# State tokens: the high and low moving parts side by side in one 512-column matmul

## The chip, the cores and the metric

The kernel runs on one NeuronCore of a Trainium2 chip. The metric is the device time of one execution in microseconds. Three runs of the kernel before gave 1387.56, 1388.13 and 1390.54 us; their median is 1388.13 us. TensorE (PE) does the matmuls, ScalarE (ACT) and VectorE (DVE) read PSUM and work in SBUF, GpSimd (POOL) works in SBUF, SyncE (SP) issues the DMAs. PEld is TensorE's loading of weights.

## The reference

Two attention reads (tokens over a state, and the state over the tokens) are joined to 8 x 544 tokens of 512 features: for each of 8 batch entries 512 ordinary tokens and 32 state tokens. Two gated layers follow.

```python
def _attn_ref(x, state):              # x 8,8,512,64; state 8,8,32,64
    a = softmax(scale * x @ state^T);   xread = a @ state
    a2 = softmax(scale * state @ x^T);  sread = a2 @ x
    return concatenate([xread, sread], axis=2)
def _moe_ref(x, w_gate, w_val, w_out):        # 512 -> 1536 -> 512
    gate = 1.0 / (1.0 + exp(-(x @ w_gate)))
    return (gate * (x @ w_val)) @ w_out
def _moe2_ref(x, w_in, w_out):                # 512 -> 2048 -> 512
    h = x @ w_in
    g = where(h >= 1, h, where(h <= -1, 0, (h + 1)**2 / 4))
    return g @ w_out
```

The 8 x 32 = 256 state tokens go through the same two layers as the 4096 others; in the kernel they are block `B` (number 8), beside blocks 0 to 7 of 512 tokens each.

## The kernel before

All matrix products are made in a reduced 32-bit type. Each factor is split into a high part (rounded, an ACT copy) and a low part (the rest, a subtraction), and a product is three matmuls that add up in PSUM: high weights by high values, high weights by low values, low weights by high values (`mm3`, lines 213 to 218, and the same three in `out1`, lines 769 to 771). Every matmul has its own load of 128x128 weights. An ordinary block gives 512 moving columns to a matmul, which fills a PSUM bank; the state block gives 256 and half a bank.

The state block appears in four places, and the change touches the first three.

- **First layer, gate and value** (`emit_g1s`, 12 units m): 8 terms of `mm3` write the two banks of one PSUM tile; then ACT takes the sigmoid of one bank (line 845), DVE multiplies by the other (846), and ACT and DVE split the product into high and low (128, 129).
- **First layer, output** (`out1` with b = 8, 12 units): 4 terms of three matmuls into four accumulating banks. `state_block` runs these units between ordinary blocks 6 and 7: it emits `emit_g1s(m)` and its eviction, and then the output of unit m - 2 (`LAG`). After unit 11, ACT copies two banks out and DVE the other two (lines 776, 778), and SP stores them.
- **Second layer, input** (`unit_s`, 8 units, four in each of two state blocks "s"): two banks of 4 terms each; each bank then goes through ACT relu, ACT square, and DVE min/max which reads the bank once more (`act_g2`, lines 1083 to 1087).
- The second layer's output for the state tokens uses other loops, which stay as they are.

Instructions run on each engine in the order in which the program emits them. The second layer's input runs over ten blocks (ordinary 0, 1, 2, state, ordinary 3, and this twice, for two halves of the hidden units). An ordinary block has 4 units (`unit`), each of seven products of six 512-column matmuls in the order `PO` = M1, M6, M5, M7, M2, M3, M4. They use four banks, u0 to u3, of two buffers each: M1 in u0, M6 in u1, M5 in u2, M7 in u3; M2 adds on top of M1's bank, M3 on M5's, M4 on M7's (line 1108). ACT copies M1's bank to SBUF after M1 (line 1133), and VectorE's sums follow from that copy. `unit_s` takes its two banks from u0 and u1, so the unit two places further on has to wait until a bank has been read. A tick after each product or half unit issues planned work of other blocks, such as the ACT copy of 128x1024 values that makes the high part of the next block (line 1044) and the POOL subtraction that makes the low part (1047).

Of the kernel before, what the change touches and what calls it, by code (L numbers as in the profile page):

```python
# [8 lines left out]
F32 = mybir.dt.float32  # L9
F32R = mybir.dt.float32r  # L10
U32 = mybir.dt.uint32
I32 = mybir.dt.int32
AF = mybir.ActivationFunctionType
ALU = mybir.AluOpType
# [11 lines left out]
def attention_moe_moe_kernel(  # L26
# [28 lines left out]
    nc = tc.nc  # L55

    ctx.enter_context(tc.manual_schedule())
    B, H, S, D = x.shape
# [5 lines left out]
    NM1 = F1 // 128  # L64
    NM2 = F2 // 128
    NQ = NM1 // 2
    NSB = B * N
    HP = H // 2
    SCALE = 1.0 / float(D) ** 0.5
    LAG = 2  # L70
# [11 lines left out]
    def ps_tile(k):  # L82
        return psets[k].tile([128, 2, 512], F32, tag="ps", name=f"ps{k}")
# [26 lines left out]
    xs_dram = tc.dram_tile([128, 4, NSB], F32, name="xs_dram")  # L110
    wf_dram = [tc.dram_tile([128, 512], F32, name=f"wf_dram_{i}") for i in range(4 * NQ)]
    ws_dram = [tc.dram_tile([128, 4, 2, 512], F32, name=f"ws_dram_{q}") for q in range(NQ)]
    y_dram = [
        tc.dram_tile([128, 4, S if j < B else NSB], F32, name=f"y_dram_{j}")
        for j in range(B + 1)
    ]
# [7 lines left out]
    def f32(ap):  # L124
        return ap.bitcast(F32)

    def split(hi, lo, src):
        nc.scalar.activation(out=hi, in_=src, func=AF.Copy)
        nc.vector.tensor_tensor(out=lo, in0=src, in1=f32(hi), op=ALU.subtract)
# [83 lines left out]
    def mm3(ps, terms):  # L213
        n = len(terms)
        for i, (wh, wl, vh, vl) in enumerate(terms):
            nc.tensor.matmul(out=ps, lhsT=wh, rhs=vh, start=(i == 0), stop=False)
            nc.tensor.matmul(out=ps, lhsT=wh, rhs=vl, start=False, stop=False)
            nc.tensor.matmul(out=ps, lhsT=wl, rhs=vh, start=False, stop=(i == n - 1))

    xa_t, xT_t, sc_t, t_t, e2_t, r2_t = {}, {}, {}, {}, {}, {}
    at_t, a_t = {}, {}
# [475 lines left out]
    wo_t = {}  # L699
# [22 lines left out]
    hr_t, h_t, acc_t = {}, {}, {}  # L722
# [36 lines left out]
    def out1(b, m, hi, lo, n, os):  # L759
        k = b % 2  # L760
        if m == 0 and os[0] == 0:
            acc_t[1, b] = [ps_tile(k) for _ in range(2)]
        acc = acc_t[1, b]
        wh, wl = wo_t[m]
        for o in os:
            c = slice(128 * o, 128 * o + 128)
            first, last = m == 0, m == NM1 - 1
            ps = acc[o // 2][:, o % 2, :n]
            nc.tensor.matmul(out=ps, lhsT=wh[:, c], rhs=hi, start=first, stop=False)  # L769
            nc.tensor.matmul(out=ps, lhsT=wh[:, c], rhs=lo, start=False, stop=False)  # L770
            nc.tensor.matmul(out=ps, lhsT=wl[:, c], rhs=hi, start=False, stop=last)  # L771
        if m == NM1 - 1 and os[-1] == 3:
            for i in range(2):
                evv = ev_tile(i)[:, :, :n]
                if i == 0:
                    nc.scalar.activation(out=evv, in_=acc[i][:, :, :n], func=AF.Copy)
                else:
                    nc.vector.tensor_copy(evv, acc[i][:, :, :n])
                nc.sync.dma_start(out=y_dram[b][:, 2 * i : 2 * i + 2], in_=evv)

    def ev_tile(i):
        if b_last:
            return hp_.tile([128, 2, 512], F32, tag=("xs_hi", "xs_lo")[i], name="ev1")
        return evp.tile([128, 2, 512], F32, tag="ev1", name="ev1", bufs=2)

    b_last = False

    def output1(bg, slot, between=None):

# [42 lines left out]
    def emit_g1s(m):  # L832
        q, mm = m // 2, m % 2
        t = ws_t[q]
        ps = ps_tile(1)
        for v in range(2):
            c = slice(256 * v + 128 * mm, 256 * v + 128 * mm + 128)
            mm3(
                ps[:, v, :NSB],
                [(t[:, r, 0, c], t[:, r, 1, c], xs_hi[:, r], xs_lo[:, r]) for r in range(4)],  # L840
            )

        def evac():
            sg = hsp.tile([128, NSB], F32, tag="sgs", name="sgs", bufs=2)
            nc.scalar.activation(out=sg, in_=ps[:, 0, :NSB], func=AF.Sigmoid)
            nc.vector.tensor_tensor(out=sg, in0=sg, in1=ps[:, 1, :NSB], op=ALU.mult)
            hi = hsp.tile([128, NSB], F32R, tag="hs_hi", name="hs_hi", bufs=3)
            lo = hsp.tile([128, NSB], F32R, tag="hs_lo", name="hs_lo", bufs=3)
            split(hi, lo, sg)
            h_t[1, B, m] = (hi, lo)  # L850

        return evac

# [5 lines left out]
    def tt(eng, o, a, b, op=SUB):  # L859
        eng.tensor_tensor(out=o, in0=a, in1=b, op=op)  # L860
# [219 lines left out]
    def act_g2(o, s, c):  # L1080


        nc.scalar.activation(out=s, in_=c, func=AF.Relu, bias=half, scale=0.5)  # L1083
        nc.scalar.activation(out=s, in_=s, func=AF.Square)  # L1084
        return lambda: nc.vector.scalar_tensor_tensor(  # L1085
            out=o, in0=s, scalar=1.0, in1=c, op0=ALU.min, op1=ALU.max
        )
# [10 lines left out]
    def u_bank(k):  # L1098
        return psu.tile([128, 512], F32, tag=f"u{k}", name=f"u{k}", bufs=2)
# [62 lines left out]

    def unit_s(m, tick):
        w = w_t[m]
        ps = [u_bank(e)[:, :NSB] for e in range(2)]
        bt = st_t["raw_c"].rearrange("p l (k f) -> p l k f", k=4)
        dt = st_t["d_c"].rearrange("p l (k f) -> p l k f", k=4)
        for e in range(2):
            terms = ((M5, bt, 0), (M4, dt, 0)) if e else ((M1, bt, 0), (M2, bt, 2))
            mm3(  # L1170
                ps[e],
                [
                    tuple(w[:, l, WI[j], 128 * k : 128 * k + 128] for l in range(2))
                    + (y[:, 0, o + k], y[:, 1, o + k])
                    for j, y, o in terms
                    for k in range(2)
                ],
            )
            if e == 0:
                tick(0)  # L1180
        late(None)
        sg = tmp.tile([128, 2, NSB], F32, tag="sg", name="sg", bufs=4)
        for e in range(2):
            act_g2(sg[:, e], sg[:, e], ps[e])()
        tick(1)
        puts.append(store_g2(B, m, sg))

# [223 lines left out]
    for w in PRE:  # L1411
        c, n = w[0], int(w[1:]) if w[1:].isdigit() else 0
# [212 lines left out]
    while wsq:  # L1625
# [8 lines left out]

    st_sb = ExitStack()
    hp_ = pool("hp1", side="right", stack=st_wo)
    xs_hi, xs_lo = (
        hp_.tile([128, 4, NSB], F32R, tag=f"xs_{n}", name=f"xs_{n}") for n in ("hi", "lo")
    )
    nc.sync.dma_start(out=f32(xs_lo), in_=xs_dram)  # L1640
    evp = hsp = pool("hsp", side="right", stack=st_sb)
    wsps = [pool("wsp", side="right", stack=st_sb)]
    st_e = ExitStack()
# [10 lines left out]

    def slot2(n, k):
        if n == 10:
            nc.scalar.activation(out=xs_hi, in_=f32(xs_lo), func=AF.Copy)
            tt(nc.vector, xs_lo, f32(xs_lo), f32(xs_hi))
        if 8 <= n < 72 and n % 8 == 0:
            load_ws((n - 8) // 32, (n - 8) // 8 % 4)  # L1660
        if n < 70:
            if n % 2 == 0 and n >= 6 and wi_steps:
                wi_steps.pop(0)()
        elif n == 70:
            st_g.close()
            wsps.append(pool("wsp2", stack=st_g))
        elif n < 72:
            for j in range(4):
                load_ws(2, j)
        elif early:  # L1670
            early.pop(0)()

    def state_block(b):
        nonlocal b_last, wtp
        if b != 6:
            return
        assert not wi_steps
        for m in range(NM1 + LAG):
            if m < 2:
                for j in range(2):  # L1680
                    load_ws(3, 2 * m + j)
            elif m < 6 and m % 2 == 0:
                for j in range(4):
                    load_ws(m // 2 + 3, j)
            evac = emit_g1s(m) if m < NM1 else None
            if evac:
                evac()
            if m >= LAG:
                hi, lo = h_t.pop((1, B, m - LAG))
                out1(B, m - LAG, hi, lo, NSB, (0, 1, 2, 3))  # L1690
        st_sb.close()
        st_g.close()
        b_last = True
        wtp = pool("wtp")
        hcps.append(pool("hcp0"))
        pe = pool("yce", stack=st_e)
        y_pools.update({i: pe for i in range(3)})
        loads, sums = load_y(0, nc.vector)
        ld, wh, wl = (
            [lambda m=m, f=f: f(m) for m in range(4)] for f in (load_wi, high_wi, low_wi)  # L1700
        )
        h3 = splits_y(0, range(7), nc.vector)[:3]
        yh = [lambda f=f: lows.append(f()) for f in h3]
        yl = lambda: lows.pop(0)()
        early.extend([*ld[:2], *loads, ld[2], wh[0], lambda: (wl[0](), ld[3]()), wh[1], wl[1]])
        early.extend([lambda: None, *sums, wh[2], yh[0], wl[2], wh[3], wl[3]])
        early.extend([lambda: (yh[1](), yl()), lambda: (yh[2](), yl()), yl])
# [16 lines left out]
    tmp = pool("tmp", side="right")  # L1724
# [179 lines left out]
```

## Time and profile before

| | |
|---|---|
| median of 3 runs | 1388.13 us (1387.56 to 1390.54) |
| the profiled execution | 1390.13 us |
| its span, first to last instruction | 1388.3 us |
| PE busy in the span | 1365.3 us (98%) |
| DVE, ACT, POOL busy | 886.7, 740.4, 263.4 us |
| mean granted TensorE clock | 0.998 of full speed |

Busy time of an engine is the time in which at least one of its instructions runs. Matmuls overlap, so the cost of one in a row of matmuls is the distance from one start to the next, not the duration that the profile gives it. Line numbers (L216) are those of the kernel before.

### The profile page before, as it was taken

To read this page: it belongs to the slowest core of one execution; us is meant where nothing else is said; L and a number is where in the kernel's file an instruction comes from. 1 tells how busy PE (TensorE), PEld (TensorE's weight loads), DVE (VectorE), ACT (ScalarE), POOL (GpSimd) and SP (SyncE) were. 2 spreads that over 40 slices of the span, in tenths; PEclk is the share of its full clock that TensorE was granted. 3 is DMA by queue.
4 is the path that set the end of the run, shared out by engine and by line. 5 is a ranking of instruction groups with operands and counts; after the bars stand their busy time and mean duration, and the time that the engine had idled before them with its cause. 6 is when DMAs were issued, how large, how long until landed. Compare 5 with 4: busy or idle time off the path is not lost. (4 is left out here: it accounts for less than half of the span.)

```text
span 1388.3 us, 23228 instructions
## 1 busy us (share of the span) xinstructions
PE 1365.3 (98%) x9028; PEld 1163.6 (84%) x9028; DVE 886.7 (64%) x1296; ACT 740.4 (53%) x1097; POOL 263.4 (19%) x163
## 2 busy tenths in 40 slices
PE   7999999999999999999999999999999999999997
PEld 5677788787777778889888888888889999999997
DVE  6667676684455454542486656666578887877775
ACT  7655556664544442321367787787875343434432
POOL 3100000000000000000047787797740000000000
PEclk9999999999999999999999999999999999999999
DMA  8387897969766858897665559966378344343333
GB/s 265 124 285 252 283 310 236 310 220 334 241 224 257 298 216 283 334 338 272 225 235 196 204 192 326 329 227 250 134 255 325 122 132 143 123 151 122 121 109 92
DMA packets 151998, 315.58 MB, mean 227 GB/s; under 512 B 13136, under 2 KB 80720, under 8 KB 150352
## 3 DMA queue, kind: packets, MB, share of 16 engines
q1 hardware_dynamic: 150536, 312.79, 64.5%
q8 instruction: 71, 1.16, 0.4%
q10 hardware_dynamic: 1352, 1.31, 0.3%
q14 instruction: 39, 0.32, 0.1%
HBM read 183.50 MB, written 130.55 MB: 226 GB/s over the span
## 5 line engine op out<-in xcount | busy, mean ns | idle before, releaser
L1125 PE MATMUL u<-yc,wt 128*128 128x512 f32 x1344 | 305.5, 389 | 0.3 <-DVE sg L1103 0.3
L1125 PEld LDWEIGHTS u<-yc,wt 128*128 128x128 f32 x1344 | 252.0, 188 | 52.9 <-DVE sg L1103 0.7
L615 PE MATMUL ps<-at_hi,M 128*128 128x512 f32 x768 | 243.5, 393 | 0.5 <-ACT at_hi L394 0.5
L615 PEld LDWEIGHTS ps<-at_hi,M 128*128 128x128 f32 x768 | 144.1, 188 | 49.9 <-issue 19.3
L860 POOL TENSOR_TENSOR w2c<-w2c 128x256 f32<-128x256 f32 (+2 forms) x40 | 40.3, 1022 | 682.3 <-DMA w2c<-w_dram 670.9
L615 PE MATMUL ps<-at_lo,M 128*128 128x512 f32 x384 | 149.9, 390 | 1.8 <-DVE at_lo L399 1.8
L769 PE MATMUL ps<-oh_hi,wo 128*128 128x512 f32 x368 | 147.1, 400 | 0.0
L770 PE MATMUL ps<-oh_lo,wo 128*128 128x512 f32 x368 | 143.7, 390 | 0.2 <-DVE oh_lo L738 0.2
L771 PE MATMUL ps<-oh_hi,wo 128*128 128x512 f32 x368 | 143.5, 390 | 0.0
L1193 PE MATMUL o<-wt,hc 128*128 128x256 f32 x476 | 135.0, 284 | 1.4 <-DVE cu L1324 0.8
L1195 PE MATMUL o<-wt,hc 128*128 128x256 f32 x476 | 134.8, 283 | 0.7 <-DVE hc L1242 0.7
L1195 PE MATMUL o<-w,hc 128*128 128x256 f32 x476 | 134.9, 283 | 0.0
L1193 PE MATMUL o<-w,hc 128*128 128x256 f32 x476 | 134.7, 283 | 0.0
L1194 PE MATMUL o<-w,hc 128*128 128x256 f32 x476 | 134.7, 283 | 0.0
L1194 PE MATMUL o<-wt,hc 128*128 128x256 f32 x476 | 134.7, 283 | 0.0
L1238 ACT ACTIVATE hc<-hc 128x512 fp32r<-128x512 f32 (+1 forms) x108 | 64.9, 603 | 130.2 <-DMA hc<-hd_dram 120.4
L600 DVE TENSOR_TENSOR M<-ps,M 128x1024 fp32r<-128x1024 f32 x48 | 56.6, 1219 | 99.7 <-ACT M L594 99.7
L1047 POOL TENSOR_TENSOR yc<-yr,yc 128x1024 fp32r<-128x1024 f32 x49 | 116.5, 2420 | 4.4 <-ACT yc L1044 4.3
L1085 DVE SCALAR_TENSOR_TENSOR sg<-u,sg 128x512 f32<-128x512 f32 x96 | 66.3, 691 | 68.1 <-ACT u L1084 67.3
L1238 ACT ACTIVATE hc<-hs 128x512 fp32r<-128x512 f32 (+1 forms) x144 | 80.0, 598 | 52.7 <-DVE hs L1235 52.1
L738 DVE TENSOR_TENSOR oh_lo<-oh_lo,oh_hi 128x1024 fp32r<-128x1024 f32 x48 | 58.6, 1223 | 73.7 <-ACT oh_hi L736 73.6
L1083 ACT ACTIVATE u<-sg,half 128x512 f32<-128x512 f32 x96 | 66.5, 692 | 67.1 <-DVE sg L1103 65.1
(165 smaller groups left out, 2755.9 us busy)
## 6 DMA issues: line engine op xcount, KB each, us to landing
hd_dram<-sg SPq DMA_DIRECT2D x64, 512.0 KB, 5.2
h_dram<-sg SPq DMA_DIRECT2D x48, 512.0 KB, 4.0
oh_lo<-h_dram SPq DMA_DIRECT2D x48, 512.0 KB, 6.0
hc<-hd_dram SPq DMA_DIRECT2D x96, 256.0 KB, 4.2
yr<-y_dram SPq DMA_DIRECT2D x32, 512.0 KB, 6.6
wraw<-in_moe_w_out_dram SPq DMA_DIRECT2D x28, 512.0 KB, 5.4
ws_dram<-w SPq DMA_DIRECT2D x24, 512.0 KB, 5.5
ws<-ws_dram SPq DMA_DIRECT2D x24, 512.0 KB, 9.7
```

The source lines that it names most:

```text
L615: nc.tensor.matmul(out=ps[bp][:, b2], lhsT=M[:, l, b2, c], rhs=a[:, b2], start=(hq == 0 and j == 0), stop=(hq == 1 and j == 2),)
L769: nc.tensor.matmul(out=ps, lhsT=wh[:, c], rhs=hi, start=first, stop=False)
L770: nc.tensor.matmul(out=ps, lhsT=wh[:, c], rhs=lo, start=False, stop=False)
L771: nc.tensor.matmul(out=ps, lhsT=wl[:, c], rhs=hi, start=False, stop=last)
L1047: low_on.tensor_tensor(out=t[:, 1, :n], in0=src, in1=f32(t[:, 0, :n]), op=SUB)
L1083: nc.scalar.activation(out=s, in_=c, func=AF.Relu, bias=half, scale=0.5)
L1085: return lambda: nc.vector.scalar_tensor_tensor(out=o, in0=s, scalar=1.0, in1=c, op0=ALU.min, op1=ALU.max)
L1125: nc.tensor.matmul(out=pm[j], lhsT=a, rhs=b, start=not more and k == 0 and i == 0, stop=k == 1 and i == 2, skip_group_check=more,)
L1193: nc.tensor.matmul(out=ps, lhsT=wh, rhs=vh, start=start and i == 0, stop=False)
L1194: nc.tensor.matmul(out=ps, lhsT=wh, rhs=vl, start=False, stop=False)
L1195: nc.tensor.matmul(out=ps, lhsT=wl, rhs=vh, start=False, stop=last)
L1238: nc.scalar.activation(out=get(j)[0], in_=raw(j), func=AF.Copy)
```

## The change

For the state block, the high and the low values lie side by side in one tile, `[128, 2, ..., 256]`. A term is now two matmuls instead of three: one of 512 columns, high weights by high and low values, which fills a whole bank, and one of 256 columns, low weights by high values, which adds into the bank's first half. The bank's second half then holds high weights by low values, and the two halves are added when the bank is read: ACT copies the first half to SBUF, DVE adds the second half to it (`fold`). In `unit_s` the activation reads this sum in SBUF where it read the bank; the sum's tile takes the two buffers that `unit` uses for the copy of M1 (tag `m1`).

```diff
+    def mm2(ps, terms):
+        n = len(terms)
+        for i, (wh, wl, v) in enumerate(terms):
+            nc.tensor.matmul(out=ps, lhsT=wh, rhs=v, start=(i == 0), stop=False)
+            nc.tensor.matmul(
+                out=ps[:, :NSB], lhsT=wl, rhs=v[:, 0], start=False, stop=(i == n - 1)
+            )
+    def fold(o, ps):
+        nc.scalar.activation(out=o, in_=ps[:, :NSB], func=AF.Copy)
+        nc.vector.tensor_tensor(out=o, in0=ps[:, NSB:], in1=o, op=ALU.add)
...
+    def out1_s(m, h):
+        if m == 0:
+            acc_t[1, B] = [ps_tile(0) for _ in range(2)]
+        wh, wl = wo_t[m]
+        for o in range(4):
+            c = slice(128 * o, 128 * o + 128)
+            ps = acc_t[1, B][o // 2][:, o % 2]
+            nc.tensor.matmul(out=ps, lhsT=wh[:, c], rhs=h, start=m == 0, stop=False)
+            nc.tensor.matmul(
+                out=ps[:, :NSB], lhsT=wl[:, c], rhs=h[:, 0], start=False, stop=m == NM1 - 1
+            )
+        if m == NM1 - 1:
+            for i in range(2):
+                acc = acc_t[1, B][i]
+                t = ev_tile(i)
+                evv = t[:, :, :NSB]
+                nc.scalar.activation(out=evv, in_=acc[:, :, :NSB], func=AF.Copy)
+                nc.vector.tensor_tensor(out=evv, in0=acc[:, :, NSB:], in1=evv, op=ALU.add)
+                nc.sync.dma_start(out=y_dram[B][:, 2 * i : 2 * i + 2], in_=evv)
...
@@ emit_g1s
-            mm3(
-                ps[:, v, :NSB],
-                [(t[:, r, 0, c], t[:, r, 1, c], xs_hi[:, r], xs_lo[:, r]) for r in range(4)],
-            )
+            mm2(ps[:, v], [(t[:, r, 0, c], t[:, r, 1, c], xs[:, :, r]) for r in range(4)])
 
         def evac():
-            sg = hsp.tile([128, NSB], F32, tag="sgs", name="sgs", bufs=2)
-            nc.scalar.activation(out=sg, in_=ps[:, 0, :NSB], func=AF.Sigmoid)
-            nc.vector.tensor_tensor(out=sg, in0=sg, in1=ps[:, 1, :NSB], op=ALU.mult)
-            hi = hsp.tile([128, NSB], F32R, tag="hs_hi", name="hs_hi", bufs=3)
-            lo = hsp.tile([128, NSB], F32R, tag="hs_lo", name="hs_lo", bufs=3)
-            split(hi, lo, sg)
-            h_t[1, B, m] = (hi, lo)
+            sg = hsp.tile([128, 2, NSB], F32, tag="sgs", name="sgs", bufs=2)
+            for v in range(2):
+                fold(sg[:, v], ps[:, v])
+            nc.scalar.activation(out=sg[:, 0], in_=sg[:, 0], func=AF.Sigmoid)
+            nc.vector.tensor_tensor(out=sg[:, 0], in0=sg[:, 0], in1=sg[:, 1], op=ALU.mult)
+            h = hsp.tile([128, 2, NSB], F32R, tag="hs", name="hs", bufs=3)
+            split(h[:, 0], h[:, 1], sg[:, 0])
+            h_t[1, B, m] = h
...
@@ unit_s
-        ps = [u_bank(e)[:, :NSB] for e in range(2)]
+        ps = [u_bank(e) for e in range(2)]
...
-            mm3(
+            mm2(
                 ps[e],
...
-                    + (y[:, 0, o + k], y[:, 1, o + k])
+                    + (y[:, :, o + k],)
...
         sg = tmp.tile([128, 2, NSB], F32, tag="sg", name="sg", bufs=4)
+        c = tmp.tile([128, 2, NSB], F32, tag="m1", name="c", bufs=2)
         for e in range(2):
-            act_g2(sg[:, e], sg[:, e], ps[e])()
+            fold(c[:, e], ps[e])
+            act_g2(sg[:, e], sg[:, e], c[:, e])()
```

Besides, `xs_hi` and `xs_lo` become one tile `xs`, and the eviction tile of the last block takes that tile's place.

## Rows read from the trace of the kernel before

**Rows 1.** The page: busy time, share of the span and instructions of each engine.
```profile
PE 1365.3 (98%) x9028; PEld 1163.6 (84%) x9028; DVE 886.7 (64%) x1296; ACT 740.4 (53%) x1097; POOL 263.4 (19%) x163
```

**Rows 2.** Busy time by stretch: first layer's state block, then the two of the second.
```profile
core 0: us, PE busy (x) PEld busy (x) DVE busy (x) ACT busy (x) POOL busy (x), PEclk, DMA share, GB/s
620.00:672.00 52.00, 52.00 (x435) 51.96 (x434) 11.39 (x25) 10.17 (x27) 0.00 (x0) 1.00 0.53 197
818.60:830.40 11.80, 11.80 (x99) 11.72 (x98) 5.04 (x10) 11.51 (x22) 11.80 (x6) 1.00 0.53 180
982.40:994.20 11.80, 11.80 (x99) 11.72 (x98) 5.09 (x10) 11.51 (x22) 11.80 (x6) 1.00 0.36 135
```

**Rows 3.** Groups by line on PE: busy, mean ns | idle before them.
```profile
L216 PE MATMUL ps<-xs_hi,ws 128*128 128x256 f32 x96 | 27.2, 283 | 0.0
L216 PE MATMUL u<-yc,wt 128*128 128x256 f32 x64 | 18.1, 283 | 0.0
L769 PE MATMUL ps<-hs_hi,wo 128*128 128x256 f32 x48 | 13.6, 283 | 0.0
```

**Rows 4.** Timeline of PE (start, duration): 256-column and 512-column matmuls.
```profile
656.14 0.28 PE L216 MATMUL ps<-xs_hi,ws 128*128 128x256 f32 x1
659.02 0.28 PE L769 MATMUL ps<-hs_hi,wo 128*128 128x256 f32 x1
...
674.05 0.39 PE L769 MATMUL ps<-oh_hi,wo 128*128 128x512 f32 x1
678.13 0.39 PE L769 MATMUL ps<-oh_hi,wo 128*128 128x512 f32 x1
```

**Rows 5.** Timeline of PE around the second layer's first state block.
```profile
818.89 0.28 PE L216 MATMUL u<-yc,wt 128*128 128x256 f32 x1
...
830.40 10.84 PE L1125 MATMUL u<-yc,wt 128*128 128x512 f32 x47
```

**Rows 6.** Timeline of ACT in that block and the two ordinary units after it.
```profile
821.84 0.47 ACT L1083 ACTIVATE sg<-u,half 128x256 f32<-128x256 f32 x1
822.34 0.42 ACT L1084 ACTIVATE sg<-sg 128x256 f32<-128x256 f32 x1
822.66 0.46 ACT L1083 ACTIVATE sg<-u,half 128x256 f32<-128x256 f32 x1
823.15 0.42 ACT L1084 ACTIVATE sg<-sg 128x256 f32<-128x256 f32 x1
823.48 1.99 ACT L1044 ACTIVATE yc<-yr 128x1024 fp32r<-128x1024 f32 x2
825.38 0.45 ACT L1083 ACTIVATE sg<-u,half 128x256 f32<-128x256 f32 x1
...
827.00 1.04 ACT L1044 ACTIVATE yc<-yr 128x1024 fp32r<-128x1024 f32 x1
827.95 0.45 ACT L1083 ACTIVATE sg<-u,half 128x256 f32<-128x256 f32 x1
...
831.99 0.60 ACT L1133 ACTIVATE m<-u 128x512 f32<-128x512 f32 x1 [0.46 <-PE u L1125]
836.80 0.69 ACT L1083 ACTIVATE u<-sg,half 128x512 f32<-128x512 f32 x1 [4.21 <-DVE sg L1103]
...
846.32 0.70 ACT L1083 ACTIVATE u<-sg,half 128x512 f32<-128x512 f32 x1 [3.62 <-DVE sg L1103]
```

**Rows 7.** Timeline of DVE there.
```profile
821.96 0.69 DVE L1085 SCALAR_TENSOR_TENSOR sg<-u,sg 128x512 f32<-128x512 f32 x1 [1.47 <-ACT u L1084]
822.79 0.42 DVE L1085 SCALAR_TENSOR_TENSOR sg<-sg,u 128x256 f32<-128x256 f32 x1
823.61 0.42 DVE L1085 SCALAR_TENSOR_TENSOR sg<-sg,u 128x256 f32<-128x256 f32 x1 [0.39 <-ACT sg L1084]
```

**Rows 8.** Timeline of POOL there.
```profile
819.17 14.26 POOL L1047 TENSOR_TENSOR yc<-yr,yc 128x1024 fp32r<-128x1024 f32 x6
```

**Rows 9.** Timeline: the eviction of the last gate and value unit (m = 11).
```profile
667.54 0.28 PE L218 MATMUL ps<-xs_hi,ws 128*128 128x256 f32 x1
667.93 0.38 ACT L845 ACTIVATE sgs<-ps 128x256 f32<-128x256 f32 x1 [3.03 <-PE ps L218]
668.34 0.42 DVE L846 TENSOR_TENSOR sgs<-sgs,ps 128x256 f32<-128x256 f32 x1 [2.99 <-ACT sgs L845]
668.80 0.42 ACT L128 ACTIVATE hs_hi<-sgs 128x256 fp32r<-128x256 f32 x1 [0.49 <-DVE sgs L846]
669.25 0.43 DVE L129 TENSOR_TENSOR hs_lo<-sgs,hs_hi 128x256 fp32r<-128x256 f32 x1 [0.48 <-ACT hs_hi L128]
```

**Rows 10.** ACT's line 267, the second bank of a tile whose first DVE reads.
```profile
L267 ACT ACTIVATE sT<-ps x1: 601/601/601, 212.4 to 212.4; 128x512 f32<-128x512 f32 x1
  DVE sT L266: 1.9, 1
```

**Rows 11.** Timeline: after the first layer's state block, and ACT before the second layer.
```profile
671.47 0.60 ACT L776 ACTIVATE ev<-ps 128x512 f32<-128x512 f32 x1 [2.25 <-PE ps L771]
672.19 0.69 DVE L778 COPY ev<-ps 128x512 f32<-128x512 f32 x1 [2.51 <-PE ps L771]
...
703.49 1.03 ACT L776 ACTIVATE ev<-ps 128x1024 f32<-128x1024 f32 x1 [4.02 <-PE ps L771]
```

More of the change, by code (lines that the diff above doesn't have):

```diff
@@ L779, in out1 @@
                 nc.sync.dma_start(out=y_dram[b][:, 2 * i : 2 * i + 2], in_=evv)
+    def out1_s(m, h):
[17 more added lines that the diff above has]
+                nc.sync.dma_start(out=y_dram[B][:, 2 * i : 2 * i + 2], in_=evv)
     def ev_tile(i):
         if b_last:
-            return hp_.tile([128, 2, 512], F32, tag=("xs_hi", "xs_lo")[i], name="ev1")
+            if i == 0:
+                last_ev.append(hp_.tile([128, 2, 2, 512], F32, tag="xs", name="ev1"))
+            return last_ev[-1][:, i]
         return evp.tile([128, 2, 512], F32, tag="ev1", name="ev1", bufs=2)
     b_last = False
+    last_ev = []
     def output1(bg, slot, between=None):
@@ L1636, in attention_moe_moe_kernel @@
     hp_ = pool("hp1", side="right", stack=st_wo)
[L1637 to L1640, printed above, removed]
+    xs = hp_.tile([128, 2, 4, NSB], F32R, tag="xs", name="xs")
+    nc.sync.dma_start(out=f32(xs[:, 1]), in_=xs_dram)
     evp = hsp = pool("hsp", side="right", stack=st_sb)
@@ L1656, in slot2 @@
         if n == 10:
-            nc.scalar.activation(out=xs_hi, in_=f32(xs_lo), func=AF.Copy)
-            tt(nc.vector, xs_lo, f32(xs_lo), f32(xs_hi))
+            nc.scalar.activation(out=xs[:, 0], in_=f32(xs[:, 1]), func=AF.Copy)
+            tt(nc.vector, xs[:, 1], f32(xs[:, 1]), f32(xs[:, 0]))
         if 8 <= n < 72 and n % 8 == 0:
@@ L1688, in state_block @@
             if m >= LAG:
-                hi, lo = h_t.pop((1, B, m - LAG))
-                out1(B, m - LAG, hi, lo, NSB, (0, 1, 2, 3))
+                out1_s(m - LAG, h_t.pop((1, B, m - LAG)))
         st_sb.close()
```

## The prediction

> **What bounds the kernel now.** I read the page's engine table first: PE is busy for 1365.3 of 1388.3 us [rows 1]. Busy time alone can mislead, because matmuls overlap, so I went on to the three stretches in which the state tokens are worked on [rows 2]. PE fills all three without a gap (52.00 of 52.00 us, 11.80 of 11.80 twice) at the full granted clock, and the groups by line show no idle time before the state matmuls [rows 3]. So the time of these stretches is matmuls times their distance, as long as nobody makes PE wait. The second thing to read in [rows 2] is who is close behind PE. In the first layer's block ACT is busy for 10 of 52 us and DVE for 11: much room. In the second layer's two blocks ACT is busy for 11.51 of 11.80 us: none. The change takes time from PE and gives work to ACT and DVE, so these two short blocks decide.
>
> **Part 1: fewer matmuls.** The distance from start to start: 24 matmuls of 256 columns from 656.14 to 659.02 us give 0.120 us each; 18 of 512 columns from 674.05 to 678.13 give 0.2267 [rows 4]. The columns of a term stay 768, but three starts become two. A term took 3 x 0.120 = 0.360 us and will take 0.2267 + 0.120 = 0.3467, if each length keeps its own distance in the mixed order. No row shows that order over a long stretch. Bounds: if the pair costs as much as before, the gain is nothing; if a 256 beside a 512 costs only half of 0.2267, the pair is 0.340 and the gain 0.020. I take 0.0133, the nearest to both rows. There are 96 + 64 + 48 = 208 terms, the counts of the three lines that begin a term [rows 3]. Gain on PE: 208 x 0.0133 = 2.8 us (0 to 4.2). No weight load was waited for in these groups, so the 208 loads that go have no price beyond this.
>
> [...]
>
> **Part 2: the second layer's state blocks.** One unit now costs ACT a relu and a square for each of two banks, from start to start 0.50 and 0.32 us (821.84, 822.34, 822.66, 823.15, 823.48 [rows 6]): 1.64 us per unit. DVE's part ran beside it, and ACT never waited for it. After the change the chain for a bank goes ACT copy, DVE add, ACT relu, ACT square, DVE min/max, and ACT's queue is in order: it stands still from the copy until DVE's add is done. Prices: from ACT's read of a 128x256 bank to the DVE operation that follows from it 0.41 us (667.93 to 668.34), from that to the next ACT operation 0.46 (668.34 to 668.80) [rows 9]. First bank: 0.41 + 0.46 + 0.50 + 0.32 = 1.69. In the second one DVE is still at the min/max of the first, which starts 0.45 after the square (822.34 to 822.79 [rows 6, 7]) and lasts 0.42; the add then starts about 0.50 after the copy instead of 0.41: 1.78. Sum 3.47; I take c = 3.5 us per unit, where ACT needed 1.64 and PE gives 8 x 0.3467 = 2.77.
>
> Now run the block. The first copy starts at 821.84 as the relu did. DVE holds a 0.69 us operation from 821.96 [rows 7], so the first add is some 0.34 late. Four units: 14.0 us. Three ACT splits of the next block stand between them in the queue and cost 1.90 (823.48 to 825.38) and 0.95 (827.00 to 827.95) [rows 6]. Together 821.84 + 0.34 + 14.0 + 2.85 = 839.03. Then comes the next unit's copy of M1 (0.60 us; before at 831.99), done at 839.7 with 0.05 to the next engine (0.46 less 0.42, rounded up). PE's product M2 adds into the bank that this copy reads (line 1108), so M2 cannot start earlier. If nothing stopped it, PE would leave the block at 818.89 + 32 x 0.3467 = 829.98 (before 830.40, [rows 5]), and M2, four products of six 512-column matmuls later (5.44), would start at 835.42. The loss is 839.7 - 835.42 = 4.3 us.
>
> PE meets it in pieces. Unit 3 needs the first bank of unit 1, whose copy starts at 821.84 + 0.34 + 3.5 + 1.90 = 827.58 and whose add ends 0.83 later, at 828.4: PE, due at 827.2, waits 1.2. The next ordinary unit's M1 needs the first bank of unit 2, free at 827.58 + 3.5 + 0.95 + 0.83 = 832.9, so PE, due at 829.98, is 2.9 late by then, and M2 takes it to 4.3. In general the loss is 4c - 9.7. The second block is the same in all its rows, 163.9 us later [rows 2]: together 8.6 us. Later in that ordinary unit ACT is still some 1 us behind its old place against PE, and it stood idle for 4.21 and 3.62 us in the two units after the block [rows 6]; I take nothing more there.
>
> Bounds of c: with no wait on DVE at all, six ACT steps of 0.33 to 0.50, 2.3 us, and no loss; with every step end to end, 4.6 us and a loss of 8.7 per block. The rows have the very steps, so I stay at 3.5, with 3.2 to 3.8 as its own range.
>
> POOL makes the low parts from those later ACT splits. Its six operations of 2.4 us fill 819.17 to 833.43 [rows 8]; the last split now ends at about 832, so its low part at 834.5, and PE wants it for the seventh product, after 839. Hidden; without that cover it would cost 1 us per block.
>
> **Part 3: the first layer's state block.** ACT and DVE have room, and two units lie between an eviction and its use, so the longer eviction costs nothing until the end. There, PE has only two output units of 4 x 0.3467 = 1.39 us after the last gate unit before it needs that unit's values. Before, the eviction began 0.39 us after the last matmul's start and its fourth step ended at 669.68, or 2.14 us after that start [rows 9]. Now there are eight steps. How far they overlap depends on whether ACT may read one bank of the tile while DVE reads the other. Line 267 answers: ACT's read of the second bank of such a tile waited 1.9 us until DVE had read the first [rows 10]. So copy, add, copy, add in turn, with 0.39 + 0.41 + 0.46 + 0.41 to the second add; then sigmoid beside it, product at 2.10, high at 2.56, low at 3.01 to 3.43. PE wants it at 0.12 + 2.77 = 2.89 after the same start: 0.6 us of waiting with the step to PE. If the copies could overlap the adds it would be 0.2; if the steps are slower, 1.
>
> [...]
>
> After it, both halves of the output go through ACT and then DVE (0.60 and 0.69 us, [rows 11]) instead of one each. The stores of SP come about 1 us later, and with them the loads queued behind: hidden, since ACT stands idle 4.02 us just before the second layer begins [rows 11]. Without that cover: 1 us. The joint tile for the input parts only moves addresses.
>
> **Sum.** -2.8 + 2 x 4.3 + 0.6 = +6.4 us. The profiled execution took 1390.13 us, 1.8 more than its span, and would take 1396.5; it is 2.0 above the median of the runs, 1388.13, against which I forecast **1394.5 us**.
>
> **Rivals.** (a) *The sums are hidden and the change does what it says.* Each block loses nothing if c is at most 2.43, and the whole comes out even at c = 2.7. Then 1388.1 - 2.8 + 0.6 = 1385.9, or 1385.3 without the last wait. For it: PE is the bound of every other stretch, and the activation reads SBUF instead of the bank, which frees the bank earlier (after two steps instead of three). Against it: ACT was at 11.51 of 11.80 us. (b) *PE waits, but about what it gains*: c near 2.9, perhaps by closer overlap on DVE and ACT, a loss of 1.9 per block, so -2.8 + 3.8 + 0.6, 1389.7. (c) *PE gains nothing from the pair*: the 512-column matmul with two strided halves runs slower, or the following 256 pays for it. With the pair at 0.360, M2 is due at 835.84 and each block loses 3.9: 1388.1 + 7.8 + 0.6 = 1396.5; with the pair at 0.370 the 144 terms of the first layer add 1.4: 1397.9. (d) *The lag spreads*: ACT's delay reaches the loads and splits at the end of the second block's half; 2 to 4 us on top, 1397 to 1399.
>
> **How the numbers follow.** Forecast 0.65, (a) 0.13, (b) 0.09, (c) 0.06, (d) 0.07. The forecast's own range, c from 3.2 to 3.8 with PE's gain between 1.5 and 4, is 1391 to 1398; the range for 8 in 10 reaches down into (b) and up over (d): 1389.5 to 1399. A difference below 0.2% (2.8 us) cannot be told from no change here. Slower by more: the forecast, (c), (d) and a little of (b), 0.78; within: most of (b) and part of (a), 0.11; faster by more: the rest of (a), 0.11.
>
> **What would show it.** Right: in the changed profile, waits of PE at the second-layer state matmuls and at line 1125's successor on DVE's additions in `fold`, then one of M2 on ACT's copy, 8 to 9 us in all; a gap on ACT of about 0.46 us before each relu; starts 0.347 us apart per pair of state matmuls. Wrong: no PE waits near 819 to 845 us, or a pair at 0.36 or 0.33, or waits of PE elsewhere.

## The result, and the profile after

The changed kernel takes 1405.85 us (median of 4 runs, 1405.47 to 1406.42) against 1388.0 for the kernel before (1387.56 to 1390.54 in the same runs): a ratio of 1.0126, 95% interval 1.0114 to 1.0138. The forecast was 1394.5 us, with a range of 1389.5 to 1399. The direction was right and the size was not: 17.9 us more instead of 6.4.

In the page of the changed kernel PE has 208 matmuls less and its span is 16.1 us longer (the view of [rows 1] again; line numbers from here on are those of the kernel whose trace is read):

```profile
span 1404.4 us, 22918 instructions
...
PE 1368.9 (97%) x8820; PEld 1153.6 (82%) x8820; DVE 913.1 (65%) x1337; ACT 756.2 (54%) x1138; POOL 263.4 (19%) x163
```

To see where the time went, take the starts of a few matmuls on PE's timeline in both kernels and compare the stretches between them.

| Stretch | before, us | after, us | difference |
|---|---|---|---|
| to the first layer's state block | 620.15 | 618.19 | -1.96 |
| that block | 51.84 | 51.60 | -0.24 |
| from it to the second layer's first state block | 146.90 | 146.93 | 0.03 |
| first state block to the second one | 163.86 | 173.24 | 9.38 |
| second one to the second layer's output | 50.19 | 59.08 | 8.89 |
| the rest | 355.36 | 355.36 | 0.00 |

The first line lies ahead of everything that was changed and varies from run to run (618.2 to 620.2 in the runs below). The loss is 9.4 and 8.9 us in the two places where [rows 2] showed ACT without room. PE's waits there, of which the kernel before has none, are (who waited, for whom, us in total, times, longest):

```profile
PE u L225 <- DVE c L232: 9.0, 6, 2.0
PE u L1158 <- ACT m L1166: 1.9, 2, 1.2
PE u L1158 <- DVE c L232: 1.9, 3, 1.0
```

These are the waits that the forecast named: state matmuls and the next unit's M1 (line 1158) for `fold`'s addition (line 232), then M2 for ACT's copy. They add up to 12.8 of the 18.3 us, for two reasons: the list counts a wait from the end of the matmul before it, so that each costs more than it says (in the first layer 0.49 listed and 0.75 lost, see part 3 below), and in the second block matmuls at a lower granted clock (0.80 and 0.50, rival C below) fill some of the time.

The surprise stands on DVE's timeline in the first block (the view of [rows 7] again; L1118 is the min/max, L232 the addition):

```profile
820.39 0.41 DVE L232 TENSOR_TENSOR c<-u,c 128x256 f32<-128x256 f32 x1
821.84 2.58 DVE L1118 SCALAR_TENSOR_TENSOR sg<-sg,c 128x256 f32<-128x256 f32 x1 [1.03 <-ACT sg L1117]
824.34 0.41 DVE L232 TENSOR_TENSOR c<-u,c 128x256 f32<-128x256 f32 x1
825.78 0.43 DVE L1118 SCALAR_TENSOR_TENSOR sg<-sg,c 128x256 f32<-128x256 f32 x1 [1.03 <-ACT sg L1117]
...
829.39 2.34 DVE L1118 SCALAR_TENSOR_TENSOR sg<-sg,c 128x256 f32<-128x256 f32 x1 [1.03 <-ACT sg L1117]
831.66 0.41 DVE L232 TENSOR_TENSOR c<-u,c 128x256 f32<-128x256 f32 x1
833.10 0.43 DVE L1118 SCALAR_TENSOR_TENSOR sg<-sg,c 128x256 f32<-128x256 f32 x1 [1.03 <-ACT sg L1117]
```

The same operation on the same 256 elements takes 0.43 us or 2.58. POOL's timeline of the same stretch (the view of [rows 8] again) says when:

```profile
817.00 7.13 POOL L1080 TENSOR_TENSOR yc<-yr,yc 128x1024 fp32r<-128x1024 f32 x3
826.77 4.68 POOL L1080 TENSOR_TENSOR yc<-yr,yc 128x1024 fp32r<-128x1024 f32 x2 [2.64 <-ACT yc L1077]
834.10 2.39 POOL L1080 TENSOR_TENSOR yc<-yr,yc 128x1024 fp32r<-128x1024 f32 x1 [2.64 <-ACT yc L1077]
```

The min/max of 821.84 begins inside a subtraction of POOL that ends at 824.13, and ends at 824.42. The one of 829.39 begins inside one that ends at 831.45, and ends at 831.73. Those of 825.78 and 833.10 find POOL idle. ACT's second relu of the first unit waits for the addition behind the first of them (ACT, the view of [rows 6] again):

```profile
821.71 0.37 ACT L231 ACTIVATE c<-u 128x256 f32<-128x256 f32 x1
824.79 0.51 ACT L1116 ACTIVATE sg<-c,half 128x256 f32<-128x256 f32 x1 [2.71 <-DVE c L232]
```

Before the change the min/max read its square from SBUF and the other input from the bank. Now both inputs are in SBUF. That gives the theory to be tested.

**Theory P:** a min/max with two SBUF inputs stands still until the POOL operation in progress ends (a stand, from here on). The queue order that the forecast priced costs some 4 us per block, and these stands cost the other 5.

**Rivals:** **Q**, the queue order is the whole loss and was priced too low; **F**, folding costs wherever it stands, the first layer too; **C**, the lower granted clock of the second block, which the windows of the changed kernel show (stretch, busy times of PE, PEld, DVE, ACT, POOL, then the clock):

```profile
996.00:1000.00 4.00, 2.85 (x15) 1.98 (x14) 2.42 (x3) 1.94 (x4) 1.37 (x1) 1.00 0.01 2
1000.00:1004.00 4.00, 2.34 (x8) 1.65 (x8) 1.79 (x2) 2.35 (x5) 3.99 (x2) 0.80 0.18 66
1004.00:1008.00 4.00, 2.65 (x9) 2.13 (x8) 2.15 (x4) 2.14 (x4) 1.37 (x2) 0.50 0.10 37
```

There PE's granted clock was 0.80 and then 0.50; in the first of these stretches, still at 1.00, PE had been busy for 2.85 of 4.00 us.

### The profile page after: what moved, and what is told of

It is laid out like the page before. It is cut to its first block, busy times and chain, and to the rows that moved or that the text cites. A ratio compares the mean times of both kernels' runs of the same rounds, so it can differ in the third digit from the quotient of the medians.

```text
span 1404.4 us, 22918 instructions
## 1 busy us (share of the span) xinstructions
PE 1368.9 (97%) x8820; PEld 1153.6 (82%) x8820; DVE 913.1 (65%) x1337; ACT 756.2 (54%) x1138; POOL 263.4 (19%) x163
## 5 line engine op out<-in xcount | busy, mean ns | idle before, releaser
L1118 DVE SCALAR_TENSOR_TENSOR sg<-u,sg 128x512 f32<-128x512 f32 x96 | 66.3, 691 | 67.3 <-ACT u L1117 66.5
L748 ACT ACTIVATE oh_hi<-oh_lo 128x1024 fp32r<-128x1024 f32 x48 | 50.6, 1056 | 93.8 <-PE ps L783 54.8
```

The source lines that it names most:

```text
L1118: return lambda: nc.vector.scalar_tensor_tensor(out=o, in0=s, scalar=1.0, in1=c, op0=ALU.min, op1=ALU.max)
```

## The experiments

**The first layer alone** (`l1_only`): `unit_s` put back.

```diff
...                                         # and mm2 back to mm3
-            fold(c[:, e], ps[e])
-            act_g2(sg[:, e], sg[:, e], c[:, e])()
+            act_g2(sg[:, e], sg[:, e], ps[e])()
```

> Only the first layer's state block is changed; the second layer's state units stay as before. Theory P (the lost time lies in the second layer, where the min/max on VectorE now has both inputs in SBUF and stands behind GpSimd's subtractions): 144 terms gain 0.36 - 0.353 = 0.007 us each, 1.0 us, less one wait of 0.5 us: 1387.5 us, -0.5 against before (-1.5 to +0.5). Rival F (the folding costs wherever it stands, because ScalarE and VectorE wait for each other): a third or more of the 17.9 us stays, 1394 or more.

1388.36 us, ratio 1.0003 (0.9994 to 1.0012); the block takes 51.60 us, as in the changed kernel. The folding there costs nothing that can be measured, and gains nothing: F is wrong.

**The second layer alone** (`us_only`): the kernel before with the changed `unit_s`, `mm2` and `fold`.

> Only the second layer's state units are changed. Theory P: the whole loss, 9.4 + 8.9 us of the two blocks: 1406 us (1404.5 to 1407.5), PE waiting 13 us in the two blocks. Rival F: two thirds of it, 1400 or less.

1405.91 us, ratio 1.0128 (1.0112 to 1.0143): the whole loss. In this run the granted clock stayed at 1.00 through both blocks (0.998 over the span), with the same two stretches of 173.2 and 59.1 us; PE's waits there add up to 15.0 us, where 13 were expected. So C is out: the slow clock of the changed kernel fell on time in which PE would have waited anyway. The single runs of the two kernels say the same: the four with a mean clock of 0.995 or 0.996 took 1405.47 to 1406.20 us, the four at 0.998 1405.58 to 1406.61.

**The sum written back into the bank** (`sum_in_bank`): as many operations, in the same order, and the min/max reads one input from SBUF.

```diff
-            fold(c[:, e], ps[e])
-            act_g2(sg[:, e], sg[:, e], c[:, e])()
+            h = ps[e][:, :NSB]
+            nc.scalar.activation(out=c[:, e], in_=h, func=AF.Copy)
+            nc.vector.tensor_tensor(out=h, in0=ps[e][:, NSB:], in1=c[:, e], op=ALU.add)
+            act_g2(sg[:, e], sg[:, e], h)()
```

> As the changed kernel, but VectorE writes the sum of the halves back into the bank's first half, and the activation and the min/max read it there: the same number of operations in the same order, the min/max with one input in SBUF instead of two. Theory P: all 16 min/max at 0.42 us (8 of them were 1.0 to 2.6), the second layer's two blocks lose what the queue order alone costs, some 4 us each, plus up to 0.6 because a bank is freed later: 1396.5 us (1395 to 1398). Rival Q (the order copy, add, relu, square, min/max in two queues is the whole loss, and the long min/max only overlap it): 1405 to 1407, as the changed kernel. Rival C (PE's lower granted clock in the second block makes the difference): the first block would lose 9 us as before, the second 4 or 5; 1401.

1396.72 us (1395.86 to 1398.55), ratio 1.0063 (1.0049 to 1.0077). The min/max of the changed kernel and of this one, by line (duration in ns, least, median, greatest):

```profile
L1118 DVE SCALAR_TENSOR_TENSOR sg<-sg,c x16: 425/426/2581, 821.8 to 1014.9; 128x256 f32<-128x256 f32 x16
```

```profile
L1118 DVE SCALAR_TENSOR_TENSOR sg<-sg,u x16: 420/422/422, 822.1 to 1005.4; 128x256 f32<-128x256 f32 x16
```

All stands are gone, and with them 9.1 of 17.9 us. Q is wrong as the whole. What is left, 168.23 - 163.86 = 4.4 us in the first block and 54.53 - 50.19 = 4.3 in the second, is the share of the queue order. PE's wait is now for the min/max, which holds the bank (3.9 us listed at the state matmuls, 1.0 at the next unit's matmuls).

**The placement alone** (`before_two_sbuf`): the kernel before, where only the second input of the min/max is changed from the bank to SBUF. The three operations of `act_g2` are written out, and the min/max takes the square twice, so the kernel leaves out the maximum with the bank's value.

```diff
-            act_g2(sg[:, e], sg[:, e], ps[e])()
+            nc.scalar.activation(out=sg[:, e], in_=ps[e], func=AF.Relu, bias=half, scale=0.5)
+            nc.scalar.activation(out=sg[:, e], in_=sg[:, e], func=AF.Square)
+            nc.vector.scalar_tensor_tensor(
+                out=sg[:, e], in0=sg[:, e], scalar=1.0, in1=sg[:, e],
+                op0=ALU.min, op1=ALU.max,
+            )
```

> The kernel before, with one thing changed: in the second layer's state units the min/max takes its square twice, both inputs from SBUF, instead of the square and the bank (so the function for the state tokens is left out in part). Theory P: of the 16 min/max some half stand at 1 to 2.6 us instead of 0.42, ending when a GpSimd subtraction ends; nothing on PE waits for them, since the bank is now free after the relu, so the time stays within 1 us of before. Rival Q: all 16 at 0.42, time as before.

```profile
L1186 DVE SCALAR_TENSOR_TENSOR sg<-sg x16: 410/2028/2629, 822.1 to 999.6; 128x256 f32<-128x256 f32 x16
```

Before, the 16 took 0.422 us each; with two SBUF inputs their median is 2.03, and the place of that input is all that the edit changes on DVE. The time was not quite as expected: 1390.19 us, ratio 1.0013 (1.0004 to 1.0022). Eight min/max in a row held DVE from 822.12 to 836.40, so the next unit's sums were late and M3 waited 1.1 us for one of them; all the loss, 1.4 us in the trace, lies in this first block. I had overlooked that queue.

**POOL that writes and doesn't read** (`pool_writes`): the changed kernel, in which POOL fills the low parts of the block after each state block with zeros (the kernel leaves out that subtraction; POOL's other work stays).

```diff
+                if fill:                    # true for ordinary block 3
+                    low_on.memset(f32(t[:, 1, :n]), 0.0)
+                    return
```

> As the changed kernel, but for the ordinary block that follows each state block GpSimd fills the low parts with zeros instead of subtracting (the low parts of that block are left out): GpSimd writes SBUF and reads nothing. Theory P (the min/max with two SBUF inputs stands behind a GpSimd operation that reads SBUF): the min/max go back to 0.42 us but for one or two beside the sums of weights that GpSimd still makes at the end of the first block (1.0); 1396.5 us (1395 to 1398.5). Rival W (any GpSimd work holds VectorE): min/max over 1 us in the same number as there are fills beside them; 1399 or more.

1396.64 us (1396.23 to 1397.92), ratio 1.0062 (1.0046 to 1.0077): the value of `sum_in_bank`, by the opposite end of the same pair. All 16 min/max, with both inputs in SBUF, are short again (group by line: us busy, mean ns of one, idle ahead of them):

```profile
L1121 DVE SCALAR_TENSOR_TENSOR sg<-sg,c 128x256 f32<-128x256 f32 x16 | 6.8, 425 | 16.4 <-ACT sg L1120 16.4
```

The fills, on POOL's timeline of this kernel (start, span of six):

```profile
815.95 5.46 POOL L1081 MEMSET yc<- 128x1024 f32 x6
```

The run can't settle W: the fills are short (0.9 us each) and were over at 821.41, before the first min/max at 822.30, so it shows that the stands go when POOL's subtractions go, not what a POOL that only writes would do. The expectation left one or two min/max at 1.0 us beside the sums of weights that POOL still makes, and none came. The one that begins among the four sums (827.97 to 831.30 on POOL's timeline) starts at 829.49 and keeps its 0.42 us, where the changed kernel's at 838.13 took 1.01 among its own four (836.44 to 839.74). Why they differ is not shown.

**Copies and additions first** (`first_in_bank`): as `sum_in_bank`, but both banks are folded before the first relu.

```diff
         for e in range(2):
             ...                             # copy, then add into the bank
+        for e in range(2):
             act_g2(sg[:, e], sg[:, e], ps[e][:, :NSB])()
```

> As the changed kernel, but in a state unit both copies and both additions come first, with the sum written back into the bank, and only then relu, square and min/max. What is left after the wait on GpSimd is gone was put down to ScalarE standing still from each copy to its addition. Theory P: a unit then costs ScalarE 2.5 us instead of 3.5, below PE's 2.8; the loss left is that of a bank that comes free only after its min/max: 1 to 2.5 us per block, 1391 us (1389 to 1393.5). Rival Q (the two queues trade waits however they are ordered): 1395 or more.

1392.26 us (1391.8 to 1393.03), ratio 1.0032 (1.002 to 1.0044). From the first copy of one unit to the first step behind it ACT needs 825.62 to 828.12 = 2.5 us instead of 3.4 (825.67 to 829.11 in `sum_in_bank`), and the blocks lose 2.1 us each. Theory P for the remainder holds for half of it: ACT standing still from copy to addition.

**Four banks** (`four_banks`): in addition, odd units take u2 and u3.

```diff
-        ps = [u_bank(e) for e in range(2)]
+        ps = [u_bank(2 * (m % 2) + e) for e in range(2)]
```

> As first_in_bank, but odd state units take banks u2 and u3, so a bank is wanted again four units later instead of two. Theory P: no unit waits for a bank any more, and both blocks lose 0 to 0.5 us: 1387.8 us (1386.8 to 1389.5), no difference from before. Rival Q: 1391 or more.

1389.47 us, ratio 1.0006 (0.9997 to 1.0015), just inside what was expected, and on the high side. PE waits for no bank any more, and the two blocks take 0.15 and 0.31 us more than before, so the last 2 us of each block were the banks. The stretch from the first layer's block to the second layer is 0.65 us longer in this trace (147.55 to 146.90): PE waits there for the low part of an ordinary block (0.4 us, `oh_lo`). Why that comes late here stays open.

**Longest matmuls first** (`four_grouped`): in addition, in each bank all matmuls of 512 columns before those of 256 (in the first layer's output, where a term goes to each of four banks, the four of 512 before the four of 256).

```diff
         for i, (wh, wl, v) in enumerate(terms):
             nc.tensor.matmul(out=ps, lhsT=wh, rhs=v, start=(i == 0), stop=False)
+        for i, (wh, wl, v) in enumerate(terms):
             nc.tensor.matmul(out=ps[:, :NSB], lhsT=wl, rhs=v[:, 0], ...)
```

> As four_banks, and in every bank all 512-column matmuls come first and then all of 256 columns, instead of turn by turn. In turn, a pair takes 0.353 us where the two lengths by themselves were 0.2267 and 0.120. Theory G (the extra 0.007 belongs to each change of length): a term takes 0.347, 208 terms gain 1.4 us more than four_banks: 1386.5 us (1385.5 to 1388). Rival S (it belongs to the 512-column matmul with two halves, whatever stands beside it): the same as four_banks, and 0.235 from start to start between 512-column matmuls in a row.

1389.51 us, ratio 1.001 (1.0001 to 1.0018): no gain, so this is no version that beats the kernel before. PE's timeline of the grouped kernel (start, span of four):

```profile
630.49 1.09 PE L225 MATMUL ps<-xs,ws 128*128 128x512 f32 x4
631.41 0.64 PE L227 MATMUL ps<-xs,ws 128*128 128x256 f32 x4
631.89 1.09 PE L801 MATMUL ps<-hs,wo 128*128 128x512 f32 x4
632.82 0.63 PE L805 MATMUL ps<-hs,wo 128*128 128x256 f32 x4
633.29 1.09 PE L225 MATMUL ps<-xs,ws 128*128 128x512 f32 x4
```

Four terms take 1.40 us, 0.350 each: between the 0.353 in turn and the 0.347 expected. Neither G nor S fits. The first layer's input tile `xs` has its halves apart and `hs` has them together (L225 and L801), with the same distance (0.92 and 0.93 us for four), so S's two halves are not the reason. The kernel before agrees: behind the state block its first five ordinary 512-column matmuls start 0.232 us apart (671.99 to 673.15), and the 0.2267 of [rows 4] was read behind them. The first layer's block gains 0.5 us against `four_banks` (51.25 to 51.76), and the wait for the low part of the next ordinary block, 0.4 us there, grows to 0.8; in the kernel before it was ready.

```profile
PE ps L783 <- DVE oh_lo L751: 0.8, 1, 0.8
```

## Why the prediction was wrong

**What bounds, and where it would be decided: right.** All of the loss lies in the two short blocks of the second layer, and PE's waits are the ones named.

**Part 1, fewer matmuls: twice what was measured.** The term was 208 x 0.0133 = 2.8 us. In turn, a pair takes 0.353, not 0.347 (12 pairs from 628.07 to 632.31 in the changed kernel):

```profile
628.07 0.40 PE L225 MATMUL ps<-xs,ws 128*128 128x512 f32 x1
628.30 0.28 PE L226 MATMUL ps<-xs,ws 128*128 128x256 f32 x1
...
632.31 0.40 PE L225 MATMUL ps<-xs,ws 128*128 128x512 f32 x1
```

That is 208 x 0.0067 = 1.4 us, inside the bounds of 0 to 4.2. The prediction also took the 208 loads that go as free: in [rows 2] PEld is as full as PE (51.96 of 52.00 us), and no run separates the two.

**Part 2, the second layer: this step failed.** It kept DVE's min/max at the 0.42 us of [rows 7] although the change moved its second input from the bank to SBUF; the text names that move only as an advantage, the bank that comes free earlier. In the first block the eight min/max took 8.6 us instead of 3.4, so 5.2 more, and `sum_in_bank`, without them, takes 173.24 - 168.23 = 5.0 us less there. The rest of the step held: c was priced at 3.5 us per unit and the blocks at 3.9 each against the kernel before (4.3 less PE's gain of 0.4). In `pool_writes`, where the stands are gone and PE's waits are still the ones forecast, a unit takes 3.58 us from its first addition on DVE to the next unit's (830.70 to 834.28) and the blocks lose 4.1 and 4.3. The bound of 4.6 for c was no bound, since it let steps queue but not grow; even with it the sum is -2.8 + 2 x 8.7 + 0.6, or 1403.3 us, below the 1405.85 measured.

The trace of before held the warning, at a place that the prediction didn't read. Beside POOL's sums of weights in the second layer's output, DVE subtracts one SBUF tile from another (DVE's timeline, kernel before):

```profile
1038.08 0.69 DVE L1085 SCALAR_TENSOR_TENSOR sg<-u,sg 128x512 f32<-128x512 f32 x1 [2.11 <-ACT u L1084]
1038.68 1.35 DVE L1235 TENSOR_TENSOR hs<-ht,hc 128x512 f32<-128x512 f32 x1
1040.07 1.67 DVE L1235 TENSOR_TENSOR hs<-hs,hc 128x512 f32<-128x512 f32 x1
1041.66 1.23 DVE L1235 TENSOR_TENSOR hs<-hc,ht 128x512 f32<-128x512 f32 x1
1042.81 0.68 DVE L1235 TENSOR_TENSOR hs<-hc,hs 128x512 f32<-128x512 f32 x1
```

And POOL's timeline there:

```profile
1036.93 5.41 POOL L860 TENSOR_TENSOR wt<-wt 128x512 fp32r<-128x512 f32 x4 [7.02 <-ACT wt L983]
```

The min/max of line 1085, with one input from the bank, takes its usual 0.69 us beside POOL. The three subtractions of two SBUF tiles behind it take 1.23 to 1.67, and the one after POOL's end at 1042.34 takes 0.68.

The runs agree on the pattern: 2.58 and 2.34 us for a min/max with both inputs in SBUF that begins inside one of POOL's subtractions, 0.42 with one input in the bank (`sum_in_bank`), 0.425 with both in SBUF and the subtractions gone (`pool_writes`). Why two SBUF inputs stand there and one does not is not shown, nor whether a POOL operation that only writes would hold them: the run with fills leaves that open.

**Part 3, the first layer: right, and slightly too low.** PE waited for the last unit: 0.49 us are listed, and by the starts of its matmuls it lost 0.65 and another 0.10 in the first pair behind the wait, 0.75 where 0.6 was forecast (667.52 to 668.29 and 668.74). ACT's second copy did wait for DVE's addition on the other bank (from 621.20 to 622.07, 0.87). With PE's gain at 144 x 0.0067 = 1.0 us, 0.24 us were left of the 1.3 forecast.

**Rivals and chances.** (a), no loss in the blocks, was wrong; (b), a loss of 1.9 per block, too; (d), a lag that reaches further, too, since the rest after both blocks is equal to 0.01 us. (c), no gain from the pair, was half right: the pair came out between its 0.360 and the 0.3467 of the forecast. No rival had an operation that grows, and the range ended at 1399.

## What to carry to other kernels

When an edit moves an operand from PSUM to SBUF, price the operation anew (here 0.42 us became up to 2.58 beside POOL's subtractions): look in the trace for VectorE operations with two SBUF inputs beside GpSimd work, and compare their greatest duration with their median. When a step is split over two engines with queues in order, write down the time from the first copy to the next unit's first copy on the busier one, and put it beside what the bound engine needs; here 3.5 against 2.8 was half of the loss and 2.5 took it away, but for the banks. Ask also whether the engines that take over the work have room: in the first layer they had it and the saving was 0.24 us, too little to be told from nothing; in the second they had none, and it cost 18.3.

## What had not been expected of the hardware

A 0.42 us min/max of VectorE took up to 2.63 us (`before_two_sbuf`) when both its inputs were in SBUF and GpSimd was in a subtraction of 2.4 us. A matmul of 512 columns beside ones of 256 starts the next one after 0.233 us instead of 0.2267 (a pair of 0.353 less 0.120), and four in a row after 256s are still at 0.2325 (0.93 us for four, `four_grouped`), as are the first ordinary ones behind such a block (0.232); why stays open. PE's granted clock fell to 0.50 in the second block of one run (1406.20 us), and stayed at 1.00 there in another whose waits lie in the same places (`us_only`, 1406.15 us).
